# Windowed attention and a low-rank mixer in one kernel: the down-product in four partial sums, folded and copied to four row groups from batch 3 on

## The chip, the core and the metric

The kernel runs on one core of a Trainium2 chip. The metric is the device time of one execution in microseconds; several runs are given by their median. The profile is that of one execution, taken by the hardware profiler.

## What is computed

The reference, cut to what matters:

```python
# q, k, v: (8 batches, 8 heads, 576 positions, 64)
scores = 1 / sqrt(64) * q @ k.T          # kept where 0 <= row - column < 64
x = softmax(scores) @ v                  # per batch: 576 positions x 512 channels
# U: 576 x 32, V: 32 x 576, w_ch1: 512 x 2048, w_ch2: 2048 x 512
h = x.T @ U @ V                          # mixes positions, rank 32
u = x + h.T
out = u + relu(u @ w_ch1) @ w_ch2
```

The change is about `x.T @ U @ V`. The first product (the down-product) sums over all 576 positions and gives 32 x 512 numbers a batch; the second (the up-product) makes 576 x 512 numbers of them, which are added to x.

## The kernel before, in words

All matmul operands are bf16. The 8 x 576 = 4608 positions are cut in two ways. Attention and the mixing of positions go by batch (576 positions: four and a half tiles of 128). The two large matmuls go by chunk (512 positions: four tiles); there are nine chunks, `mlp(c)`. A batch therefore begins or ends in the middle of a tile: batch 3 covers tiles 13 (its second half) to 17, batch 4 tiles 18 to 22 (its first half), and so on.

The order of the work is written out by hand. Each engine has one queue, which it works off in the order in which the program emits instructions; SP's queue only issues DMAs, and POOL's mostly does. `mlp(c)` is a list of 32 slots of four 512-column matmuls: slots 0 to 15 are the first large product (`ch1`, tile `psA`, each followed by a relu on ACT or VectorE into `c1_i`), slots 16 to 31 the second (`ch2`, tile `psU`, four slots for each of the four tiles of the chunk). The last slot of a tile ends with an addition on VectorE (`osb`, L761) and the store of the result by SP (L774). The last loop of the program goes through the slots and emits after each what the table `PLACE` puts there for batch b = c + 1. So the work of batch 3 is spread over chunk 2, that of batch 4 over chunk 3, and so on to batch 7 in chunk 6; chunks 7 and 8 have no such work.

What the table places, with its slots for batches 3 to 7 before the change:

- `S`, `M`, `PV` (slots 0 to 8): scores, masks and the product with v; ends with the divisions on VectorE into `xs` (L487 to L510).
- `U` (slot 14), function `UM`, L531 and L539: the down-product. `ub` (128 positions x 32) is the stationary operand, so one matmul fills 32 of the array's columns, and the array takes four such matmuls beside each other (column groups g = 0 to 3, rows 32 g to 32 g + 31 of the result `pshh`). Tile t of the batch goes to the groups t % 2 and t % 2 + 2, both times over all 512 channels. The fifth, half-filled tile goes to all four groups, with 256 channels each. So rows 0 to 63 of `pshh` hold two partial sums which together are the result, and rows 64 to 127 hold the same again. ACT copies the whole to `hh` in bf16 (L546).
- `V` (slot 16), function `VM` by way of `mixed`, L619: the up-product. The stationary operand is `vrep`, which has V four times, once in each group of 32 rows. A matmul takes 64 rows of `hh` and of `vrep`, and so adds the two partial sums while it multiplies. Two matmuls lie beside each other (rows 0 to 63 and 64 to 127) with two results. There are three pairs: `(4,)` (256 columns each), `(0, 1)` and `(2, 3)` (512 columns each). Six additions on VectorE (L634) then put x plus the result into the tiles `un`.
- `UT` (slots 17, 17, 18, 18, 19): the transposed copies of `un` into `uTc`, the input of `ch1`. For batches 3 to 7 these are DMA transposes on SP's queue (L649). The first `ch1` of a chunk needs all four of its tiles: chunk 3 needs the first three of batch 3, chunk 4 the first two of batch 4, chunk 5 the first two of batch 5, chunks 6 and 7 one of batches 6 and 7.

Also on SP's queue: the DMA transposes of keys and queries for a later batch (`TX`, L304, slots 20 to 24 by `CROSS_N`, slots 24 to 28 in chunk 2). POOL issues the loads of keys, queries and values (L128, L137) for later batches. Within a slot the slot's own work comes first, then `S`, `M`, `PV`, then `TX`, then `U`, `V`, `UT`. PSUM: `pshh` and the pairs of V take from `ps_big` (two tiles of two banks); `psA`, `psU` and one tile of V take turns in three single banks.

Of the kernel before, what the change touches and what calls it, by code (L numbers as in the profile page):

```python
# [9 lines left out]
ALU = mybir.AluOpType  # L10

BF16 = mybir.dt.bfloat16
FP32 = mybir.dt.float32
# [3 lines left out]
def kernel(  # L17
# [11 lines left out]
    nc = tc.nc  # L29
    B, H, S, D = q.shape  # L30
    DM = H * D
    R = moe_U.shape[1]
    F = moe_w_ch1.shape[1]
    P = nc.NUM_PARTITIONS
# [7 lines left out]
    NGR = 2  # L42
    NXB = 2
    NXT = 3
    GP = S // GR
    NFULL = S // P
    CH = 512
# [15 lines left out]
    wk_pool = ctx.enter_context(tc.tile_pool(name="wk", bufs=2))  # L63
# [42 lines left out]
    def staged(b):  # L106
        if b >= NGR:
            return kn[b % 2], qn[b % 2]
        return tuple(
            r[0:GP, :].rearrange("p (h c d) -> p h c d", h=H, c=GR) for r in (kr[b % 2], qr[b % 2])  # L110
        )
# [38 lines left out]
    def shift_low(b, copy, t):  # L150
# [9 lines left out]
        out=ident[:],  # L160
        in_=ident[:],
# [10 lines left out]
    for n, base, step, mult in ((0, 0, 1, -1), (1, -1, -1, 1), (1, W, 1, -1)):  # L172
        nc.gpsimd.affine_select(
            out=maskA[:, 0, n, :],
            in_=maskA[:, 0, n, :],
# [17 lines left out]
    for i in range(2):  # L193
        nc.vector.memset(kn[i][GP:P, NFULL, :, :], 0.0)
        nc.vector.memset(qn[i][GP:P, NFULL, :, :], 0.0)


    nc.sync.dma_start(
        out=uf[0][:, 0:NFULL, :], in_=moe_U[0 : NFULL * P, :].rearrange("(c p) r -> p c r", p=P)
# [48 lines left out]
    def uT_of(c):  # L248
        if c not in uT_tiles:
            uT_tiles[c] = uT_pool.tile([P, TPC, NDC, P], BF16, name="uTc")  # L250
        return uT_tiles[c]


    def attention(b, spare=False):
# [9 lines left out]
        kx, qx = (f.rearrange("p (t j w) -> p t j w", t=NT, j=HP) for f in (kf, qf))  # L264

        grouped = b < NGR
        turn = [0]

        def tr(src, j, wide=False):
# [6 lines left out]
            else:  # L276
                tp = ps_tp.tile([P, GR, GP], BF16, name="tpg", tag="tp")
            turn[0] += 1
            for c in range(GR):
                for g in range(2):  # L280
                    nc.tensor.transpose(  # L281
                        tp[g * D : (g + 1) * D, c, :], src[:, 2 * j + g, c, :], ident[0:GP, 0:GP]
                    )
# [233 lines left out]
        hh = {}  # L517
        xc = lambda src, t, dc: src[:, t, :, :].rearrange("p h d -> p (h d)")[:, dc * P : (dc + 1) * P]

        def UM(ts):  # L520
            def f():
                if ts[0] == 0:
                    if spare:
                        hh["ps"] = psum["spare"].tile([P, CH], FP32, name="psh", tag="spare")
                    else:
                        hh["ps"] = ps_big.tile([P, 2, CH], FP32, name="pshh", tag="big")[:, 0, :]
                for t in ts:
                    xt = x[:, t, :, :].rearrange("p h d -> p (h d)")
                    if t < 4:
                        for g in (t % 2, t % 2 + 2):  # L530
                            nc.tensor.matmul(  # L531
                                hh["ps"][g * R : (g + 1) * R, :], ub[odd][:, t, :], xt,
                                start=(t < 2), stop=False,
                            )
                        continue

                    for g in range(4):
                        cols = slice((g % 2) * CH // 2, (g % 2 + 1) * CH // 2)
                        nc.tensor.matmul(  # L539
                            hh["ps"][g * R : (g + 1) * R, cols], ub[odd][:, t, :], xt[:, cols],  # L540
                            start=False, stop=True,
                        )
                if ts[-1] == NT - 1:
                    hh["sb"] = wk_pool.tile([P, CH], BF16, name="hh", tag="hh")
                    for cs in (slice(0, CH // 2), slice(CH // 2, CH)) if spare else (slice(0, CH),):
                        nc.scalar.copy(out=hh["sb"][:, cs], in_=hh["ps"][:, cs])  # L546
            return f
# [57 lines left out]
        def VM(ts, banks=None):  # L605
            ps = {}
            cols = CH if len(ts) == 2 else CH // 2

            def up():
                if banks is None:  # L610
                    pair = ps_big.tile([P, 2, CH], FP32, name="psv", tag="big")
                    ps[0] = [pair[:, n, 0:cols] for n in range(2)]
                else:
                    ps[0] = [one[:, 0:cols] for one in banks()]
                for n in range(2):
                    half = slice(n * 2 * R, (n + 1) * 2 * R)
                    off = ts[n % len(ts)] * P + (0 if odd else W)
                    lo = 0 if len(ts) == 2 else n * cols
                    nc.tensor.matmul(  # L619
                        ps[0][n], vrep[half, off : off + P], hh["sb"][half, lo : lo + cols],  # L620
                        start=True, stop=True,
                    )

            def add(n):
                def f():
                    t = ts[n % len(ts)]
                    g = g0 + t
                    rs = slice(
                        W if (odd and t == 0) else 0, W if (not odd and t == NT - 1) else P
                    )  # L630
                    cs = slice(0, CH) if len(ts) == 2 else slice(n * cols, (n + 1) * cols)
                    if g not in u_tiles:
                        u_tiles[g] = u_pool.tile([P, DM], BF16, name="un")
                    nc.vector.tensor_tensor(  # L634
                        out=u_tiles[g][rs, cs],
                        in0=ps[0][n][rs],
                        in1=x[rs, t, :, :].rearrange("p h d -> p (h d)")[:, cs],
                        op=ALU.add,
                    )
                return f  # L640

            return [up, add(0), add(1)]

        def UT(t):
            def f():
                g = g0 + t
                dst = uT_of(g // TPC)[:, g % TPC, :, :]
                if b >= NXT:
                    nc.sync.dma_start_transpose(out=dst, in_=u_tiles[g][:])  # L649
# [59 lines left out]
    def mlp(c):  # L709
# [80 lines left out]
        "M": [0, 1, 2, 4, 5],  # L790
        "PV": [8],
        "U": [14],
        "V": [16],
        "UT": [17, 17, 18, 18, 19],
    }
    PLACE_0 = {"V": [0, 0, 1, 2, 2, 3, 4, 4, 4]}
    PLACE_1 = {
# [29 lines left out]
    def turn_over(n, cols, rows=P):  # L827
# [5 lines left out]

    turn_over(62, 96)
    att = {0: attention(0, spare=True)}
    a = att[0]
    nc.vector.tensor_scalar(
        out=maskA[:, 0, 2, :],
        in0=maskA[:, 0, 1, :],
# [6 lines left out]
        out=maskB[:, 0:3, :],  # L846
        in0=maskA[:, 0, 0:3, :],
# [56 lines left out]
    for c in range(NCH):  # L904
        slots = all_slots[c]

        def place(b, parts, where):
            if b not in att:
                att[b] = attention(b)
            for part in parts:  # L910
                for f, s in zip(att[b][part], where[part]):
                    all_slots[c + s // 100][s % 100].append(f)

        b = c + 1
# [85 lines left out]
```

The softmax here doesn't subtract the row's maximum and nothing guards it: scores larger than these inputs give would overflow.

## Time and profile before

| what | value |
|---|---|
| median of 9 runs | 313.05 us (312.71 to 315.79) |
| the profiled execution's own time | 313.05 us |
| its span, first to last instruction | 311.3 us |
| granted TensorE clock, mean | 1.000 |
| `psA` L724, TensorE | 131.2 us busy, 580 matmuls |
| `psU` L748, TensorE | 129.1 us busy, 592 matmuls |
| `pshh` L531 and L539, TensorE, 7 batches | 4.3 us (56 of 512 columns) and 2.0 us (28 of 256) |
| `psv` L619, TensorE | 5.0 us (32 of 512 columns) and 2.3 us (16 of 256) |
| `hh` L546, ACT | 587 ns each, 7 times |
| `un` L634, VectorE | 26.1 us, 48 times |
| DMA transposes `uTc` from `un`, SP's queue | 23, median 6.7 us from issue to landing |

How to read it: a busy time is the union of the instructions of one kind, so matmuls that lie beside each other count once; the end of a matmul is modelled, so a matmul of 512 columns is shown as 378 ns although the next can start after 216. In the timeline a line is a run of instructions of one kind, with start and duration in us; in brackets stand the engine's idle time before it and what ended it. "SPq" is the time that the SP queue takes to issue a DMA; when it lands is told apart.

### The profile page before, as it was taken

The page shows a single profiled execution, that of the slowest core. Times are in us where ns is not written, and L with a number is a line of the kernel's source. Part 1 is how long each engine was busy: PE and PEld are TensorE (multiplying, and loading weights), DVE is VectorE, ACT ScalarE, POOL GpSimd, SP SyncE. Part 2 cuts the span into 40 slices and gives each one's busy share as a digit, 9 for nine tenths or more (in the row PEclk, how much of TensorE's full clock was granted, in tenths as well). Part 3 has the DMA queues.
Part 4 walks back from the last instruction along what each step waited for, and adds up shares of the span by engine and source line. Part 5 has one row for each costly group of instructions (what it writes and reads, how often), then busy time and mean ns, then how long its engine had stood idle before and what let it go on. Part 6 is the DMA issues. An engine that isn't in the chain of part 4 may idle for free.

```text
span 311.3 us, 6992 instructions
## 1 busy us (share of the span) xinstructions
PE 304.5 (98%) x2919; PEld 147.3 (47%) x2919; DVE 162.6 (52%) x308; ACT 108.9 (35%) x173; POOL 101.7 (33%) x133
## 2 busy tenths in 40 slices
PE   7899999999999999999999999999999999999996
PEld 6543554544455544454445344534454444444443
DVE  4575467437758754774368435844574343016011
ACT  3655670467038510642063304340345003201500
POOL 8693263294399097029307900000000000000000
PEclk9999999999999999999999999999999999999999
DMA  7999999999999999999999997505100545010012
GB/s 102 164 208 208 207 168 151 147 140 147 129 150 154 132 145 162 181 159 154 159 163 188 170 133 169 128 32 133 69 2 0 120 180 193 27 76 34 0 64 73
DMA packets 156496, 39.88 MB, mean 128 GB/s; under 512 B 145040, under 2 KB 151440, under 8 KB 156464
## 3 DMA queue, kind: packets, MB, share of 16 engines
q0 software_dynamic: 104720, 18.88, 83.3%
q1 hardware_dynamic: 51744, 20.55, 36.0%
q8 instruction: 23, 0.38, 0.5%
q14 instruction: 9, 0.07, 0.1%
HBM read 37.97 MB, written 9.44 MB: 152 GB/s over the span
## 4 chain that ended last, share of the span: by engine, by line
PE 93%; DMA 3%; POOL 2%; issue 0%; ACT 0%; DVE 0%; POOLq 0%
PE psA L724 41%; PE psU L748 40%; DMA vA<-in_v_dram 3%; PE sc L345 3%; PE xw L407 2%; PE psv L619 2%; PE pshh L531 1%; PE tpu L653 1%; PE tpg L281 0%; POOL qr L119 0%; PE low L345 0%; PE psh L531 0%; POOL vB L151 0%; PE xr L407 0%; POOL kr L119 0%
## 5 line engine op out<-in xcount | busy, mean ns | idle before, releaser
L724 PE MATMUL psA<-uTc,w1b 128*128 128x512 bf16 (+1 forms) x580 | 131.2, 378 | 0.4 <-ACT uTc L599 0.4
L748 PE MATMUL psU<-w2b,c 128*128 128x512 bf16 (+2 forms) x592 | 129.1, 373 | 0.0
L748 PEld LDWEIGHTS <-c 128*128 128x128 bf16 x592 | 56.0, 98 | 66.4 <-issue 3.6
L724 PEld LDWEIGHTS <-w1b 128*128 128x128 bf16 x580 | 54.1, 98 | 64.4 <-issue 2.9
L736 ACT ACTIVATE c<-psA 128x512 bf16<-128x512 f32 x84 | 50.1, 597 | 88.3 <-PE psA L724 88.0
L761 DVE TENSOR_TENSOR osb<-psU,un 128x512 f32<-128x512 f32 (+2 forms) x29 | 19.5, 673 | 68.9 <-PE psU L748 68.9
L734 DVE TENSOR_SCALAR c<-psA 128x512 bf16<-128x512 f32 x60 | 41.4, 689 | 25.6 <-PE psA L724 25.6
L634 DVE TENSOR_TENSOR un<-psv,xs 128x512 bf16<-128x512 f32 (+3 forms) x48 | 26.1, 593 | 23.2 <-PE psv L619 22.9
L365 ACT ACTIVATE pts<-sc 128x1024 bf16<-128x1024 f32 x32 | 31.4, 1029 | 2.4 <-PE sc L345 2.3
L137 POOL DMA_DIRECT2D vA<-in_v_dram x32 | 28.4, 912 | 7.7 <-DMA kr<-in_k_dram 3.0
L128 POOL DMA_DIRECT2D qr<-in_q_dram x30 | 26.6, 887 | 3.8 <-PE sc L345 1.8
L128 POOL DMA_DIRECT2D kr<-in_k_dram x30 | 26.5, 883 | 3.5 <-PE tpg L281 2.0
L398 ACT ACTIVATE ptl<-low 128x256 bf16<-128x256 f32 x6 | 2.3, 384 | 62.0 <-PE high L345 62.0
L371 DVE TENSOR_TENSOR pts<-pts,maskA 128x1024 bf16<-128x1024 bf16 x28 | 19.1, 683 | 1.7 <-ACT pts L365 1.7
L922 POOL COPY held<-qf 1x1 bf16<-1x1 bf16 x5 | 0.9, 179 | 53.1 <-DMA qf<-qr 43.5
L498 DVE TENSOR_TENSOR xs<-xw,rcw 128x896 bf16<-128x896 f32 x14 | 15.3, 1092 | 0.5
L345 PEld LDWEIGHTS <-kf 64*64 64x64 bf16 x704 | 9.8, 107 | 7.6 <-issue 7.0
L345 PE MATMUL sc<-qf,kf 64*64 64x128 bf16 (+1 forms) x608 | 11.5, 212 | 0.5 <-DVE qf L298 0.3
L407 PEld LDWEIGHTS <-pts 128*64 128x64 bf16 x512 | 9.9, 110 | 3.6 <-issue 3.0
L546 ACT CAST hh<-pshh 128x512 bf16<-128x512 f32 x7 | 4.1, 587 | 13.6 <-PE pshh L539 13.5
L656 ACT COPY uTc<-tpu 128x512 bf16<-128x512 bf16 x9 | 5.3, 586 | 10.2 <-PE tpu L653 10.2
L137 POOL DMA_DIRECT2D vB<-in_v_dram x8 | 7.4, 922 | 3.4 <-DMA qr<-in_q_dram 2.4
(115 smaller groups left out, 175.8 us busy)
## 6 DMA issues: line engine op xcount, KB each, us to landing
out_dram<-osb SPq DMA_DIRECT2D x27, 256.0 KB, 2.3
vA<-in_v_dram POOLq DMA_DIRECT2D x32, 128.0 KB, 8.5
kr<-in_k_dram POOLq DMA_DIRECT2D x24, 128.0 KB, 6.1
qr<-in_q_dram POOLq DMA_DIRECT2D x24, 128.0 KB, 6.3
w2b<-in_moe_w_ch_dram POOLq DMA_DIRECT2D x4, 512.0 KB, 15.7
out_dram<-late SPq DMA_DIRECT2D x8, 256.0 KB, 3.0
vB<-in_v_dram POOLq DMA_DIRECT2D x8, 128.0 KB, 10.5
w1b<-in_moe_w_ch_dram POOLq DMA_DIRECT2D x2, 512.0 KB, 10.9
```

Source lines behind the costliest of these rows:

```text
L128: nc.gpsimd.dma_start(out=dst[0:rows, t, :, :], in_=src[b, :, t * P : t * P + rows, :].rearrange("h p d -> p h d"),)
L137: nc.gpsimd.dma_start(out=dst[:, :, 0:D], in_=v[b, :, lo : lo + P, :].rearrange("h p d -> p h d"))
L345: nc.tensor.matmul(sc[g][r0 : r0 + W, col * W : (col + n) * W], keys_of(j, u, rs), queries_of(j, blk, n, rs), start=not spare, stop=last o ...
L365: nc.scalar.activation(out=dst, in_=sc[:], func=ACT.Exp, scale=scale)
L371: nc.vector.tensor_tensor(out=dst, in0=dst, in1=maskA.rearrange("p g n w -> p g (n w)"), op=ALU.mult)
L407: nc.tensor.matmul(dst, pts[:, h // 2, h % 2, blk, :] if blk < NB - 1 else ptl[:, h // 2, h % 2, :], rhs, start=True, stop=True,)
L634: nc.vector.tensor_tensor(out=u_tiles[g][rs, cs], in0=ps[0][n][rs], in1=x[rs, t, :, :].rearrange("p h d -> p (h d)")[:, cs], op=ALU.add,)
L724: nc.tensor.matmul(ps[i][:, ts.start * P : ts.stop * P], w1b[:, dc, i * P : (i + 1) * P], uTc[:, ts, dc, :], start=(dc == 0), stop=(dc == ...
L734: nc.vector.tensor_relu(out=c1[i][:], in_=ps[i][:])
L736: nc.scalar.activation(out=c1[i][:], in_=ps[i][:], func=ACT.Relu)
L748: nc.tensor.matmul(acc[t][:, lo:hi], c1[i][:, t * P : (t + 1) * P], w2b[:, i, lo:hi], start=(i == 0), stop=(i == NFC - 1),)
L761: nc.vector.tensor_tensor(out=osb[:, lo:hi], in0=acc[t][:, lo:hi], in1=u_tiles[g][:, lo:hi], op=ALU.add,)
```

## The change

From batch 3 on (`folded`, with `NFOLD = 3`):

- Down-product: tile t goes to column group t alone, so one wave of four matmuls replaces two; the fifth tile goes to all four groups with 128 channels each. `pshh` then holds four partial sums.
- Instead of one copy by ACT: ACT copies rows 64 to 127 to `part` in fp32; VectorE adds rows 0 to 63 to it, copies rows 32 to 63 of that to `other`, adds both into rows 0 to 31 of `hh` in bf16, and copies these to rows 32 to 63 and then rows 0 to 63 to rows 64 to 127.
- Up-product: a matmul takes 32 rows. The pair `(4,)` uses row groups 0 and 1, the pair `(0, 1)` groups 0 and 1, the pair `(2, 3)` groups 2 and 3.
- The table: V from slot 16 to 18, UT from 17, 17, 18, 18, 19 to 19, 19, 20, 20, 21.

```diff
+    NFOLD = 3
...
+        folded = b >= NFOLD
...
                     if t < 4:
-                        for g in (t % 2, t % 2 + 2):
+                        for g in (t,) if folded else (t % 2, t % 2 + 2):
                             nc.tensor.matmul(
                                 hh["ps"][g * R : (g + 1) * R, :], ub[odd][:, t, :], xt,
-                                start=(t < 2), stop=False,
+                                start=(folded or t < 2), stop=False,
                             )
                         continue
 
                     for g in range(4):
-                        cols = slice((g % 2) * CH // 2, (g % 2 + 1) * CH // 2)
+                        n = 4 if folded else 2
+                        cols = slice((g % n) * CH // n, (g % n + 1) * CH // n)
...
                     hh["sb"] = wk_pool.tile([P, CH], BF16, name="hh", tag="hh")
+                    if folded:
+                        one, two = slice(R, 2 * R), slice(0, 2 * R)
+                        part = wk_pool.tile([2 * R, CH], FP32, name="part", tag="part")
+                        other = wk_pool.tile([R, CH], FP32, name="other", tag="other")
+                        nc.scalar.copy(out=part[:], in_=hh["ps"][2 * R : P])
+                        nc.vector.tensor_tensor(
+                            out=part[:], in0=hh["ps"][two], in1=part[:], op=ALU.add
+                        )
+                        nc.vector.tensor_copy(out=other[:], in_=part[one])
+                        nc.vector.tensor_tensor(
+                            out=hh["sb"][0:R], in0=part[0:R], in1=other[:], op=ALU.add
+                        )
+                        nc.vector.tensor_copy(out=hh["sb"][one], in_=hh["sb"][0:R])
+                        nc.vector.tensor_copy(out=hh["sb"][2 * R : P], in_=hh["sb"][two])
+                        return
...
                     half = slice(n * 2 * R, (n + 1) * 2 * R)
+                    if folded:
+                        q = ts[n] if len(ts) == 2 else n
+                        half = slice(q * R, (q + 1) * R)
...
-        "V": [16],
-        "UT": [17, 17, 18, 18, 19],
+        "V": [18],
+        "UT": [19, 19, 20, 20, 21],
```

## The prediction, made before the changed kernel ran

> **What bounds the kernel now.** I read the page first: engine shares and the chain that ended last.
> ```profile
> PE 304.5 (98%) x2919; PEld 147.3 (47%) x2919; DVE 162.6 (52%) x308; ACT 108.9 (35%) x173; POOL 101.7 (33%) x133
> ...
> PE 93%; DMA 3%; POOL 2%; issue 0%; ACT 0%; DVE 0%; POOLq 0%
> ```
> TensorE bounds it; its DMA and POOL shares of the chain lie in the first 20 us. Every microsecond taken off TensorE is a gain, unless a wait takes its place. So I next read batch 3 (the first changed one, in chunk 2) in order of time. TensorE and ACT:
> ```profile
> 108.57 0.62 PE L531 MATMUL pshh<-xs,ub 128*32 128x512 bf16 x8
> 109.02 0.28 PE L539 MATMUL pshh<-xs,ub 128*32 128x256 bf16 x4
> 109.23 1.04 PE L724 MATMUL psA<-uTc,w1b 128*128 128x512 bf16 x4
> 110.10 1.03 PE L748 MATMUL psU<-w2b,c 128*128 128x512 bf16 x4
> 111.06 0.71 PE L619 MATMUL psv<-hh,vrep 64*128 64x256 bf16 x6
> 111.71 0.60 PE L748 MATMUL psU<-w2b,c 128*128 128x512 bf16 x2
> ```
> ```profile
> 108.68 0.60 ACT L736 ACTIVATE c<-psA 128x512 bf16<-128x512 f32 x1 [0.27 <-PE psA L724]
> 109.35 0.59 ACT L546 CAST hh<-pshh 128x512 bf16<-128x512 f32 x1
> ```
> Columns: start, duration, engine and line. The down-product (U) holds TensorE from 108.57 to 109.23, the up-product (V) from 111.06 to 111.71. Then VectorE and the SP queue, on which the transposes `uTc<-un` of the next chunk stand:
> ```profile
> 111.38 3.40 DVE L634 TENSOR_TENSOR un<-psv,xs 128x256 bf16<-128x256 f32 x6 [3.93 <-PE psv L619]
> 114.70 0.68 DVE L761 TENSOR_TENSOR osb<-psU,un 128x512 f32<-128x512 f32 x1
> ```
> ```profile
> 112.89 6.00 SPq L649 DMA_TRANSPOSE uTc<-un  x4
> 118.99 0.53 SPq L774 DMA_DIRECT2D out_dram<-osb  x1
> 119.58 1.33 SPq L649 DMA_TRANSPOSE uTc<-un  x1
> 121.00 0.54 SPq L774 DMA_DIRECT2D out_dram<-osb  x1
> 121.64 1.27 SPq L304 DMA_TRANSPOSE kf<-kr  x1
> ```
> The first three of these transposes by the view of the tile uTc, and the start of chunk 3 on TensorE:
> ```profile
> L649 SPq DMA_TRANSPOSE uTc<-un x3: 1207/1245/1471, 112.9 to 115.6; - x3
> ...
> DMA to landing us min/median/max: 6.2/7.2/7.9
> ```
> ```profile
> 124.67 1.03 PE L724 MATMUL psA<-uTc,w1b 128*128 128x512 bf16 x4
> ```
> Chunk 3 multiplies tiles 12 to 15, and batch 3's first three transposes make 13, 14 and 15. The third lands at 115.6 + 7.9 = 123.5, only 1.2 us before TensorE wants it. This margin is hidden from the list of waits, and it decides the case.
>
> **What the change takes off TensorE.** I count from U's start (108.57 = 0). U is two waves of four 512-column matmuls, 0.22 apart, then a wave of 256 columns (0.11) and 0.10 until the next matmul in another array shape: 0.66. After: one wave of four (0.22), one of 128 columns (0.05), 0.10: 0.39. That is -0.27. V is 0.12 + 0.22 + 0.22 + 0.10 = 0.65. After, the pairs of `(0,1)` and `(2,3)` lie on different row groups and run together, while the pair of `(4,)` shares groups 0 and 1 with `(0,1)`: 0.12 + 0.22 + 0.01 + 0.10 = 0.45, -0.20. Five batches: 5 x 0.47 = -2.4 us.
> The trace has four column tiles at once (the four starts of a wave lie within 0.01 us), but of row tiles only two. The Trainium skill speaks against the full gain: "TensorE: Matmul & The Clock Gate", Measured speedup vs the span model, gives four row tiles of 512 columns 3.07 times. With 0.38 for one matmul that is 4 x 0.38 / 3.07 = 0.49 in place of 0.39, so V saves 0.10, and the sum is -1.9 us. I take the row: pairs start within 0.01 us and the next pair 0.22 later. If nothing more than now runs together, U keeps only its smaller last wave: -0.05 a batch, -0.3 in all. A loss has no cause there: there are fewer matmuls and as many changes of shape.
>
> **The fold, and when V can start.** TensorE reaches V at 0.39 (U) + 0.87 (c_15) + 12 x 0.216 (slots 16 to 18 of psU) + 0.10 = 3.95. The fold: ACT's copy keeps its place and length (a 64-row copy of 512 fp32; the row above, 0.59) and ends at 109.94, 1.37. The handover ACT to VectorE is 0.03 (ptl in this trace), between dependent VectorE operations 0.03 (rce to xs), back to TensorE 0.05. Add of PSUM and SBUF: 0.69 (`osb` rows). Copy of 512 fp32 in SBUF: no such row; between a 520-element bf16 copy (0.28) and an fp32 one out of PSUM (0.69). "VectorE: DVE Perf Modes", The perf-mode tier table, has fp32 copies at 2x, 1227 ns for 2048, from which I estimate 0.43, and take it. Second add: 0.69 (same form; the page has fp32 adds at 1x too). Two bf16 copies: 0.28 each. Sum 1.37 + 0.03 + 0.69 + 0.43 + 0.69 + 0.56 + 4 x 0.03 + 0.05 = 3.94. So without disturbance V waits for nothing, and the cover is gone to the last 0.01 us: whatever is longer is on the path. VectorE itself is idle there (3.93 us idle before un).
> The disturbance is in the trace. The SBUF copies of VectorE are longer while POOL issues DMAs:
> ```profile
> L144 DVE COPY vB<-vA x1: 830/830/830, 118.7 to 118.7; 64x1560 bf16<-64x1560 bf16 x1
> ```
> ```profile
> L144 DVE COPY vB<-vA x1: 565/565/565, 182.8 to 182.8; 64x1560 bf16<-64x1560 bf16 x1
> ```
> Over eleven such copies the excess goes from 0 to 0.38, mean 0.13. POOL issues during the fold of batches 3, 4 and 5, not of 6 and 7: three copies, +0.39 (bounds 0 and 1.1). There V starts at 4.34. Alone, the change would then give 3 x (0.39 - 0.47) + 2 x (-0.47) = -1.2.
> The PSUM pair of pshh is held until the first add (2.1) instead of 1.37; V asks for it after 3.9, so nothing waits. The bank of psU t=2 is free when the first `osb` add is done (8.66 below), and slot 24 wants it at 4.34 + 0.45 + 0.87 + 4 x 0.864 = 9.1: covered by 0.4.
>
> **What is late next: the transposes.** V moves from slot 16 to 18 and UT from 17..19 to 19..21. Slot 19's own work ends with the first `osb` add of the chunk and its store, which are emitted ahead of the slot's extras. In the built order of the SP queue the store therefore stands now ahead of all five transposes, and it waits for VectorE, which does six `un` adds first. Batch 3: V 4.34, first add 0.32 later (111.06 to 111.38), adds and osb 4.00 (111.38 to 115.38): 8.66. Handover 0.1, store's issue 0.59: first transpose at 9.35, where it was at 4.32. From first issue to third landing the trace has 112.9 to 123.5, 10.6: lands at 19.95. TensorE wanted it at 124.67 - 108.57 = 16.1. Chunk 3 begins **3.9 us later** than before (gain and fold included).
> Can it land sooner? Unloaded, in chunk 5, four transposes land 2.4 us after their issue, so three would take 2 x 1.3 + 2.4 = 5.0, and nothing would stall:
> ```profile
> L649 SPq DMA_TRANSPOSE uTc<-un x4: 1191/1212/1218, 208.9 to 212.8; - x4
> ...
> DMA to landing us min/median/max: 2.4/2.4/2.4
> ```
> But POOL issues key, query and value loads until 124.2 and the page's DMA row stays at 9 till 187 us. The loads outstanding at 118 are not fewer than at 113. Nearest row: 10.6; bounds 5.0 and 12.
> Batch 4 needs two (tiles 18 and 19). V 4.34 + 0.32 + 3.83 (143.42 to 147.25) + 0.1 + 0.65 = 9.24; first issue to second landing 144.8 to 153.3, 8.5: 17.7 against 16.1, +1.6. The loads for batch 6 follow the SP queue, which lags by 3.5 where TensorE lags by 3.9, so they are 0.4 ahead: I take **+1.4** (0 to 2). Batch 5 needs two, but its loads are all issued by 178.9, 6.2 after U's start, and gone when the transposes come at 9.2: no stall, -0.1. Batches 6 and 7 need one, unloaded: -0.47 each. On SP the key and query transposes of the batch after next are now woven in behind the second one; these are wanted a chunk later and have over 10 us to spare.
> Sum: 3.9 + 1.4 - 0.1 - 0.9 = **+4.3**. The profiled execution has a span of 311.3 and a time of 313.05, which is also the median of the runs. So a span of 315.6 and a time near 317.3; I say 317.2.
>
> **Rivals.** (1) *Transposes in time* (0.12). One mechanism: with SP silent from 113 to 118 the loads run ahead alone and the late transposes meet a free DMA. It decides where first issue to third landing is under 16.0 - 9.35 = 6.7. For it: 5.0 unloaded; against it: from 101 to 180 us every transpose took 5.5 us or more but for three issued between 162 and 166. Then the sum is -1.2: 311.9. With some of the delay: 312.5 to 315.5 (0.13, of it 0.05 under 314.0). (2) *Likeliest* (0.63): 315.5 to 318.7. (3) *The clock too* (0.07). TensorE would idle 4.0 us ahead of chunk 3. After the start its longest idle stretch in this trace is under 1 us, with PEclk at 9. "TensorE: Matmul & The Clock Gate", What's actually happening, lets an idle window of about 3.4 us halve the clock until a busy one has passed. By the row nothing happens; by the rule, as the windows run free, (4.0 - 3.4) / 3.4 = 0.18 of cases lose about half of 3.4 us, 1.7: 318.9. (4) *It does not pack* (0.05). U is 0.61 and V 0.65. Chunks 3 and 4 begin as above, since the transposes set them and V still waits for the fold; batch 5 gives 4.34 - 4.17 - 0.05 = +0.1, 6 and 7 -0.05 each: +5.3, 318.3.
>
> **Range.** 313.4 to 319.0: leaves out rival 1, a little of what lies between, and half of 3: 0.18. A measurement of this kernel tells 0.3% (0.9 us) from no change: faster 0.12, same 0.05, slower 0.83.
>
> **What would show it.** U's block 0.39 and V's 0.45 on TensorE; five VectorE operations between U and V, 2.6 to 3.1 us from end to end of the fold; the first `uTc<-un` 9 us after U, behind the store of osb; TensorE idle of some 4 us at the start of chunk 3 and 1.5 at chunk 4, released by DMA uTc, none at chunk 5 and later. Wrong if those transposes land within 6.7 us, or if the fold takes much over 3.1 us: then V itself is the wait, five times.

## The result, and the profile after

The changed kernel takes 318.39 us (median of 10 runs, 316.42 to 319.36), the kernel before 313.15 us in the same sessions (31 runs). The ratio is 1.0152, with a 95% interval of 1.0134 to 1.017: slower, by 4.8 us by the ratio and 5.2 by the medians. The profiled execution took 317.36 us, its span is 315.7.

The page of the changed kernel, its engine shares, slices, chain of waits and costliest group. Line numbers are some 21 higher than before (`psA` is L745, `psU` L769, `psv` L640, `un` L655, `uTc` L670):

```profile
PE 306.0 (97%) x2899; PEld 148.6 (47%) x2899; DVE 174.3 (55%) x333; ACT 108.7 (34%) x173; POOL 102.1 (32%) x133
...
PEclk9999999999999999599999999999999999999999
DMA  7999999999999999999957998651500166020012
...
PE 89%; DMA 5%; POOL 2%; DVE 1%; SPq 1%; issue 1%; ACT 0%; POOLq 0%
...
L745 PE MATMUL psA<-uTc,w1b 128*128 128x512 bf16 (+1 forms) x580 | 133.1, 382 | 4.1 <-DMA uTc<-un 3.7
```

TensorE is busy for longer (306.0, before 304.5) although it has 20 matmuls fewer, and 3.7 us of idle time ahead of `psA` are new, released by a transpose. The 5 in the row PEclk, slice 17 of 40 counted from 1, is the reason for the longer busy time: the granted clock was halved there. In the DMA row, slices 21 and 22 (158 to 174 us) are at 5 and 7, where they were at 9.

Batch 3 in order of time, first TensorE, then VectorE, then the SP queue, then the start of chunk 3:

```profile
108.46 0.40 PE L533 MATMUL pshh<-xs,ub 128*32 128x512 bf16 x4
108.69 0.23 PE L542 MATMUL pshh<-xs,ub 128*32 128x128 bf16 x4
108.85 1.04 PE L745 MATMUL psA<-uTc,w1b 128*128 128x512 bf16 x4
109.72 2.75 PE L769 MATMUL psU<-w2b,c 128*128 128x512 bf16 x12
112.41 0.62 PE L640 MATMUL psv<-hh,vrep 32*128 32x256 bf16 x6
```

```profile
111.72 0.28 DVE L560 COPY hh<-hh 32x512 bf16<-32x512 bf16 x1
112.03 0.55 DVE L561 COPY hh<-hh 64x512 bf16<-64x512 bf16 x1
```

```profile
116.72 0.37 SPq L795 DMA_DIRECT2D out_dram<-osb  x1
117.15 7.18 SPq L670 DMA_TRANSPOSE uTc<-un  x5
```

```profile
128.08 1.87 PE L745 MATMUL psA<-uTc,w1b 128*128 128x512 bf16 x4 [3.72 <-DMA uTc<-un]
```

U takes 0.39 from its start to the next matmul (0.66 before). V starts 3.95 after U without a wait on TensorE. The store of the first `osb` stands ahead of the transposes, as foreseen; the first transpose goes at 117.15, 8.69 after U (4.32 before). The third lands at 119.82 + 8.12 = 127.94, and 0.14 later chunk 3 begins, 19.62 after U where it was 16.10. Its first four matmuls take 1.87 us in place of 1.03: they run at half clock. TensorE in stretches of 3.41 us (start and end, length, then busy time and count of TensorE, weight loads, VectorE, ACT and POOL, the granted clock, and two columns that are not used here):

```profile
123.06:126.47 3.41, 1.30 (x7) 0.39 (x4) 0.69 (x1) 0.00 (x0) 0.00 (x0) 1.00 2.12 148
126.47:129.88 3.41, 1.80 (x5) 0.44 (x5) 0.00 (x0) 0.00 (x0) 0.00 (x0) 0.50 1.82 134
129.88:133.29 3.41, 3.41 (x59) 1.91 (x59) 1.39 (x3) 2.49 (x4) 0.00 (x0) 0.50 1.22 256
```

The wait begins at 128.08 - 3.72 = 124.36. The clock falls 2.1 us later and stays at a half for 6.83 us; from 128.08 to 133.29 TensorE works at half speed. What that costs can be read between the start of chunk 3 (128.08, before 124.67) and U of batch 4, a stretch in which nothing was changed:

```profile
140.62 0.61 PE L531 MATMUL pshh<-xs,ub 128*32 128x512 bf16 x8
```

```profile
146.44 0.40 PE L533 MATMUL pshh<-xs,ub 128*32 128x512 bf16 x4
```

It is 15.95 us before and 18.36 after: the half clock costs 2.4 us. Laid side by side, the stretches of the two kernels give this account (start of U in batch 3 to chunk 3, then chunk to chunk, in us):

| stretch | before | after | difference | predicted |
|---|---|---|---|---|
| U of batch 3 to chunk 3 | 16.10 | 19.62 | +3.52 | +3.9 |
| chunk 3 to 4 (batch 4) | 32.04 | 34.26 | +2.22 | +1.4 |
| chunk 4 to 5 (batch 5) | 32.05 | 31.71 | -0.34 | -0.1 |
| chunk 5 to 6 (batch 6) | 32.04 | 31.56 | -0.48 | -0.47 |
| chunk 6 to 7 (batch 7) | 32.04 | 31.55 | -0.49 | -0.47 |

The sum is +4.43; U of batch 3 itself comes 0.11 sooner, so +4.3, and the spans differ by 315.7 - 311.3 = 4.4. The +2.22 of batch 4 is +2.41 for the clock, ahead of its U, and -0.19 behind it.

### The profile page after: what moved, and what is told of

Its sections match the earlier page's. It is cut to its first block, busy times and chain, and to the rows that moved or that the text cites. A ratio compares the mean times of both kernels' runs of the same rounds, so it can differ in the third digit from the quotient of the medians.

```text
span 315.7 us, 6956 instructions
## 1 busy us (share of the span) xinstructions
PE 306.0 (97%) x2899; PEld 148.6 (47%) x2899; DVE 174.3 (55%) x333; ACT 108.7 (34%) x173; POOL 102.1 (32%) x133
## 4 chain that ended last, share of the span: by engine, by line
PE 89%; DMA 5%; POOL 2%; DVE 1%; SPq 1%; issue 1%; ACT 0%; POOLq 0%
PE psA L745 41%; PE psU L769 36%; DMA vA<-in_v_dram 3%; PE sc L347 3%; DMA uTc<-un 3%; PE xw L409 2%; PE psv L640 1%; DVE un L655 1%; PE pshh L533 1%; SPq L670 1%; PE tpu L674 1%; PE tpg L283 0%; PE low L347 0%; POOL qr L120 0%; POOL vB L152 0%
## 5 line engine op out<-in xcount | busy, mean ns | idle before, releaser
L745 PE MATMUL psA<-uTc,w1b 128*128 128x512 bf16 (+1 forms) x580 | 133.1, 382 | 4.1 <-DMA uTc<-un 3.7
L769 PE MATMUL psU<-w2b,c 128*128 128x512 bf16 (+2 forms) x592 | 129.1, 373 | 0.0
L745 PEld LDWEIGHTS <-w1b 128*128 128x128 bf16 x580 | 54.5, 99 | 69.2 <-issue 8.7
L769 PEld LDWEIGHTS <-c 128*128 128x128 bf16 x592 | 55.9, 98 | 65.7 <-issue 2.8
L655 DVE TENSOR_TENSOR un<-psv,xs 128x512 bf16<-128x512 f32 (+3 forms) x48 | 26.1, 593 | 4.6 <-PE psv L640 4.2
L553 DVE TENSOR_TENSOR part<-pshh,part 64x512 f32<-64x512 f32 x5 | 3.4, 683 | 12.6 <-ACT part L552 12.6
L782 DVE TENSOR_TENSOR late<-psU,un 128x512 f32<-128x512 f32 x8 | 5.3, 688 | 5.8 <-PE psU L769 5.7
```

Source lines behind the costliest of these rows:

```text
L655: nc.vector.tensor_tensor(out=u_tiles[g][rs, cs], in0=ps[0][n][rs], in1=x[rs, t, :, :].rearrange("p h d -> p (h d)")[:, cs], op=ALU.add,)
L745: nc.tensor.matmul(ps[i][:, ts.start * P : ts.stop * P], w1b[:, dc, i * P : (i + 1) * P], uTc[:, ts, dc, :], start=(dc == 0), stop=(dc == ...
L769: nc.tensor.matmul(acc[t][:, lo:hi], c1[i][:, t * P : (t + 1) * P], w2b[:, i, lo:hi], start=(i == 0), stop=(i == NFC - 1),)
L782: nc.vector.tensor_tensor(out=osb[:, lo:hi], in0=acc[t][:, lo:hi], in1=u_tiles[g][:, lo:hi], op=ALU.add,)
```

## The experiments

The theory: the move of V and UT makes the transposes late (chunk 3 waits), the wait makes the clock fall, and packing and fold gain a little in each batch. The rival: the fold itself, its VectorE work or the contention that it meets, costs the time.

**The move alone.** The kernel before, with only the table changed:

```diff
-        "V": [16],
-        "UT": [17, 17, 18, 18, 19],
+        "V": [18],
+        "UT": [19, 19, 20, 20, 21],
```

> The kernel before with V in slot 18 and UT in 19 to 21, without the fold and the four partial sums. Theory (late transposes): the first transpose goes 9 to 9.6 us after U's start, chunk 3 begins 4 us late, the clock halves for one or two windows (1.6 to 2.2 us), and nothing is gained: 319 (318.3 to 320). Rival (the fold or its contention is the cost): 313 to 313.5, as before.

Measured: 318.81 us, ratio 1.0193 (1.0173 to 1.0212). Without any fold, the start of chunk 3 looks as after:

```profile
127.72 1.86 PE L724 MATMUL psA<-uTc,w1b 128*128 128x512 bf16 x4 [3.10 <-DMA uTc<-un]
```

Chunk 3 begins 19.36 after U, +3.26; chunk 3 to 4 lasts 34.72, +2.68; the later chunks last 32.04 as before. The clock falls here too (0.50, the third column from the right):

```profile
126.64:133.47 6.83, 5.75 (x63) 2.57 (x64) 1.94 (x4) 2.49 (x4) 0.00 (x0) 0.50 1.29 194
```

Nothing but the clock is left to explain the 2.68, since nothing is packed here and no wait stands in that stretch. So the move alone costs 317.1 - 311.3 = 5.8 us of span, more than the whole change, and the rival falls.

**The transposes ahead of the store.** The changed kernel, with the first store of chunks 2 to 6 held back until the slot of the last UT is through:

```diff
-                    nc.sync.dma_start(out=outf[g * P : (g + 1) * P, lo:hi], in_=osb[:, lo:hi])
+                    store = lambda: nc.sync.dma_start(
+                        out=outf[g * P : (g + 1) * P, lo:hi], in_=osb[:, lo:hi]
+                    )
+                    if t == 0 and HOLD <= c + 1 < B:
+                        behind.append(store)
+                        continue
+                    store()
...
             for f in extra:
                 f()
+            if behind and fill is ups_21:
+                behind.pop(0)()
```

> Theory (late transposes): the loss is the transposes of un standing behind the first osb store on the SP queue. With that store behind them, the first one goes at about 6.3 us after U's start (third un add done) in place of 8.7, the third lands some 10.8 later at 17.1, and TensorE wants it at 15.5: 1.6 us of idle ahead of chunk 3, too short for half a clock, so a time of 312.7 (311.2 if the transposes also land sooner, 314 if they land later). Clock 1.0. Rival (the fold, its VectorE work or the place of V is the cost): no change, 317 to 318.5.

Measured: 312.4 us, ratio 0.9975 (0.9958 to 0.9992), 6 us under the changed kernel. The first transpose goes 6.04 after U, and what is left of the wait is small:

```profile
114.76 7.60 SPq L672 DMA_TRANSPOSE uTc<-un  x5
```

```profile
125.46 1.02 PE L747 MATMUL psA<-uTc,w1b 128*128 128x512 bf16 x4 [0.46 <-DMA uTc<-un]
```

The order on the SP queue, with what follows from it, is thus by far the most of the loss. The runs go from 310.98 to 316.01, where those of the kernel before in the same sessions go from 312.67 to 315.31. The margin is near zero, and how fast the transposes land differs between executions: in the six traces in which batch 3 is as before, the third takes 6.6 to 8.1 us. That this makes the spread is likely, but the other runs have no trace.

**The clock.** The changed kernel, with matmuls on a zero tile in the wait of chunk 3, into the bank which the first real matmul then overwrites (17 of them, in the next kernel 8):

```diff
+                if (c, ids) == (3, (0,)):
+                    for _ in range(17):
+                        nc.tensor.matmul(
+                            ps[0], idle[:, 0:P], idle[:, 0:CH], start=True, stop=True
+                        )
```

> The changed kernel with 17 matmuls on the zero tile ahead of chunk 3's first matmul, in the same bank, which the first real matmul overwrites; they fill some 3.7 us in which TensorE waits for the transposes. Theory (idleness halves the clock): chunk 3 begins as late as after (within 0.3), the granted clock is 1.0, and the time is 316.4 (316.0 to 316.9), 1.6 to 2.2 less than after. Rival (the half clock follows from something else in that stretch): clock 0.99 as before, 318.4 or a little more.

Measured: 315.86 us, ratio 1.0092 (1.0071 to 1.0112), less than after, while TensorE does 3.7 us of extra work. In its profiled execution chunk 3 begins 19.54 after U, as late as after, and the clock is full ahead of it and behind it. (The 17 matmuls end last here. The third transpose had landed two microseconds earlier, so that without them only some 1.7 us would have been idle: this trace alone proves little.)

```profile
123.00:130.50 7.50, 7.50 (x36) 3.43 (x35) 1.38 (x2) 0.00 (x0) 0.00 (x0) 1.00 1.66 185
130.50:137.00 6.50, 6.50 (x113) 3.25 (x111) 4.02 (x7) 4.40 (x7) 0.00 (x0) 1.00 0.56 105
```

The five other runs have a mean clock of 0.999 or 1.000; the 0.993 of the profiled one comes mostly from a half-clock stretch from 14.6 to 18.0, in the start of the program. So all eleven executions of the changed kernel lose clock, and with the wait filled none of six does there. The idle wait is what halves the clock, and that was worth some 2 us here (2.5 by the medians, 0.006 of 313 = 1.9 by the ratios).

> As busy_wait with 8 matmuls on the zero tile in place of 17: 1.7 us of the wait are filled, some 2.1 stay idle. After, the half clock began 2.3 us into an idle of 3.9. If a window has to be idle for most of 3.4 us, clock 1.0 and 316 as with 17. If 2 us of idle are enough, clock 0.995 and 317.5 (2.6 to 3.4 us at half clock, less what is already idle).

With 8: 316.33 us, ratio 1.0091 (1.0062 to 1.0121), neither of the two answers. Three of six runs have a clock of 0.995 and take 316.9 to 317.4, three have 0.999 or 1.000 and take 314.6 to 315.7. In the profiled one the transposes landed late, 2.85 us stayed idle, and the clock fell for 3.41 us. The two expectations had not allowed for both outcomes in one kernel; whether the length of the wait or its place decides between them, these runs do not show.

**The fold from batch 4 on.** Batch 3 keeps the old products and the old slots:

```diff
-    NFOLD = 3
+    NFOLD = 4
...
-    PLACE_3 = {**PLACE, "SV": [5, 5, 6, 6]}
+    PLACE_3 = {**PLACE, "SV": [5, 5, 6, 6], "V": [16], "UT": [17, 17, 18, 18, 19]}
```

> The change from batch 4 on; batch 3 as in the kernel before, with its old slots. Chunk 3 then begins as before, clock 1.0. If chunk 4's transposes stall as predicted for batch 4 (+1.4), the time is 313.1 + 1.4 - 0.1 - 0.9 = 313.5. If they do not, as in the changed kernel, four batches give 0.45 each: 311.3. Rival (the fold itself costs time): over 313.5.

Measured: 312.37 us, ratio 0.9984 (0.997 to 0.9999), between the two, with runs from 310.77 to 315.19. The two transposes that chunk 4 needs, and its start, in the profiled execution (312.06 us):

```profile
L670 SPq DMA_TRANSPOSE uTc<-un x2: 1283/1540/1797, 149.5 to 150.8; - x2
...
DMA to landing us min/median/max: 5.7/6.2/6.8
```

```profile
156.93 1.03 PE L745 MATMUL psA<-uTc,w1b 128*128 128x512 bf16 x4
```

They land at 156.3 and 156.5, 0.4 us ahead of TensorE: just in time here, and so probably late in the longer runs (one of them has a clock of 0.994), which have no trace. With the store also held back (both edits, from batch 4 on), that chance should go:

> The change from batch 4 on, and in its chunks the first osb store behind the transposes of un on the SP queue. With the fold from batch 4 on alone the two transposes of batch 4 landed 0.4 us before chunk 4 in the profiled run, and the runs spread from 310.8 to 315.2. Theory (these transposes are late by chance in some runs): they go 1.8 us sooner, no chunk waits, four batches give 0.45 each: 311.3, spread under 1.5 us. Rival (the spread comes from the fold): 312.4 as without it.

Measured: 311.73 us, ratio 0.9952 (0.994 to 0.9964), runs from 311.59 to 312.08. The five runs lie within 0.5 us. That fits late transposes as the source of the spread, and not the fold, but five runs are few: `fold_4_act_copy` below, in which the store is held back too, goes from 311.91 to 314.52 in 22. This version beats both kernels, by 1.6 us the one before.

**The fold from batch 5 on**, with `NFOLD = 5` and the old slots for batches 3 and 4:

> The change from batch 5 on only; batches 3 and 4 as in the kernel before with their old slots. No transposes of these batches fall into the loads' time. If packing and fold are worth what the periods of chunks 5 and 6 show after (0.48 each), three batches give 1.4: 311.7, with little spread and clock 1.0. Rival (part of what a batch gained after came from the loads having run ahead in the stall): 312.5 to 313.

Measured: 312.02 us, ratio 0.9961 (0.9948 to 0.9974), 1.3 under the 313.33 of the kernel before beside it; 1.4 was expected. Chunks 5 and 6 last 31.56 each, as in the changed kernel, so the gain of a quiet batch doesn't hang on the stall of chunk 3. Chunk 4 to 5 lasts 31.88: batch 5 gives only 0.17.

**Two row groups or four.** The same with all pairs of V on row groups 0 and 1, and without the last copy of `hh`:

```diff
-                        q = ts[n] if len(ts) == 2 else n
+                        q = n
...
-                        nc.vector.tensor_copy(out=hh["sb"][2 * R : P], in_=hh["sb"][two])
```

> The fold from batch 5 on, with all pairs of V on the first two row groups, and so without the last copy of hh. It measures what the four row groups give V. By the row of before (pairs on the same groups 0.22 apart) V is 0.65 again, and chunks 6 and 7 last 31.77 us where four groups give 31.56 and the kernel before 32.04: 0.21 between two and four groups, 312.5 in all. By the rule of 3.07 times the difference is 0.10, chunks 6 and 7 at 31.66. If the row groups give nothing, 31.56. Batch 5, whose third pair waited for the last copy, is then no slower than with four groups.

Measured: 312.21 us, ratio 0.9988 (0.9968 to 1.0007); by the time alone this is unclear, by the trace it isn't. Chunks 5 and 6 last 31.78 and 31.77, 0.21 more than with four groups. V of batch 6 on TensorE, first with two groups, then with four (`fold_from_5`):

```profile
208.37 0.71 PE L639 MATMUL psv<-hh,vrep 32*128 32x256 bf16 x6
209.01 0.82 PE L768 MATMUL psU<-w2b,c 128*128 128x512 bf16 x3
```

```profile
208.74 0.50 PE L640 MATMUL psv<-hh,vrep 32*128 32x256 bf16 x6
209.17 0.60 PE L769 MATMUL psU<-w2b,c 128*128 128x512 bf16 x2
```

Start to start 0.64 and 0.43: the four row groups give what the row of before said (0.65 and 0.45), not half of it. Batch 5 lasts 31.88, the same as with four groups: V's block is 0.76 in both, since in both the first copy of `hh` took 0.72 there (0.28 in batches 6 and 7) and V waited for it and, with four groups, for the copy behind it.

**V in its old slot.** The changed kernel with V in slot 16 and UT in 17 to 19:

> The changed kernel with V in slot 16 and UT in 17 to 19, as before. TensorE reaches V at 0.39 + 0.87 + 4 x 0.216 + 0.1 = 2.2 us after U, the fold is ready at 3.95: a wait of 1.75 in each of five batches, 8.7 us. The transposes then go ahead of the osb store and land near 17 us after U, where TensorE wants them at 15.7 + 1.75: no stall, clock 1.0. 313.1 - 2.4 + 8.7 = 319.4. Rival (the fold's wait is short or is taken back before the next chunk): under 315.

Measured: 320.7 us, ratio 1.0223 (1.0203 to 1.0243). The tile `psv` shows the wait:

```profile
  DVE hh L557: 5.3, 5
```

Five waits of 1.06 on average, released by the second add (L557) and not by the copies behind it: V's first matmul reads rows 0 to 31 of `hh` only, and starts 3.3 to 3.5 after U. The second, which elsewhere starts at the same moment, follows 0.3 to 0.4 later, after the copy to rows 32 to 63. Each wait is thus shorter than the 1.75 expected. Without a fall of the clock a batch lasts 33.2, 1.1 longer than before; but four of the five runs also lost clock, which had not been expected. So the later slot is needed for the fold, and leaving V where it was costs more than the move.

**The last copy on ACT**, in the best version (`fold_4_ut_first`):

```diff
-                        nc.vector.tensor_copy(out=hh["sb"][2 * R : P], in_=hh["sb"][two])
+                        nc.scalar.copy(out=hh["sb"][2 * R : P], in_=hh["sb"][two])
```

> The fold from batch 4 on with the store behind the transposes, and the last copy of hh (64 rows) on ACT in place of VectorE. Theory (POOL's DMA issues lengthen the SBUF copies of VectorE alone): the copy takes the same in batches 4 and 5 as in 6 and 7, some 0.5 us, and the excess of 0.26 is seen no more in this copy; since an undisturbed copy of VectorE takes 0.28, the time stays at 311.7 to 312.2. Rival (any SBUF copy beside POOL's issues is longer): ACT's copy is longer in batch 4 or 5 than in 6 and 7 by 0.2 or more.

Measured: 312.76 us, ratio 0.9992 (0.9978 to 1.0006). The tile `hh`, ACT's copy and VectorE's before it (ns, shortest, median, longest):

```profile
L563 ACT COPY hh<-hh x4: 616/616/617, 144.6 to 240.5; 64x512 bf16<-64x512 bf16 x4
```

```profile
L562 DVE COPY hh<-hh x4: 283/416/734, 143.8 to 240.2; 32x512 bf16<-32x512 bf16 x4
```

ACT's copy takes the same in all four batches, while VectorE's copy ahead of it takes 734 and 550 in batches 4 and 5, in which POOL issues DMAs, and 283 in 6 and 7. As far as two copies can show it, the excess belongs to VectorE's copies within SBUF. The time was mis-expected: the third pair waits for ACT in all four batches. V's block is 0.64 in batches 6 and 7 in place of 0.43, and 1.09 and 1.31 in 4 and 5, where VectorE's longer copies come on top. (Of the 2.9 us by which the span of this execution exceeds that of `fold_4_ut_first`, half lies behind the issue of the last store, where nothing was changed.)

## Why the prediction was right, and where its sum was not

**Direction, place and size held.** The predicted 317.2 is close to the profiled 317.36, and the range holds the median of 318.39. What bounds the kernel, the order on the SP queue and the stall of chunk 3 were read off the trace of before. But two terms of the sum, batch 4 and the clock, were wrong by about 2 us each and cancelled. That the total is so close is luck; the stall of chunk 3 is not.

**TensorE's gain** was right: U 0.39; V 0.43 in batches 6 and 7, which gave 0.48 and 0.49 for a predicted 0.47. For packing by row groups the trace's row held. The smaller gain was an estimate from the 3.07 times that the Trainium skill gives for four row tiles ("TensorE: Matmul & The Clock Gate", Measured speedup vs the span model); it would have made V 0.55.

**The fold** has the foreseen parts: 0.58 (ACT), 0.68, 0.42 (estimated at 0.43), 0.68, 0.28, 0.28 undisturbed. Wrong was "There V starts at 4.34": it starts at 3.95 in every batch. The prediction took `hh` for one thing that is ready or not; a matmul waits only for the rows it reads, and only the pair on the third and fourth row groups needs the last copy. The excess was real (the last copy took 554, 689 and 555 ns in batches 3, 4 and 5, and 287 and 289 in 6 and 7), but cost TensorE only the wait of the third pair: V's block is 0.55, 0.72 and 0.58 in batches 3, 4 and 5 against 0.43 in the quiet ones.

**The transposes of batch 3** were right: first one at 8.69 for 9.35 (the 0.39 of V is most of it), 10.8 to the third landing for 10.6, chunk 3 later by 3.5 for 3.9. `place_only` and `ut_first` show the cause from both sides.

**Batch 4, "+1.4", failed.** There was no stall: from U of batch 4 to chunk 4 it takes 15.90, 0.19 less than before. The step that failed is "The loads for batch 6 follow the SP queue, which lags by 3.5". The queue did lag by 3.5: the key and query transpose on whose landing POOL waits was issued at 129.23 before and at 132.77 now. But it landed 8.1 us behind its issue before, and 4.0 in the changed kernel, so POOL's wait ended earlier and the loads did not lag. Before, then after:

```profile
129.23 1.28 SPq L304 DMA_TRANSPOSE qf<-qr  x1
```

```profile
137.47 0.18 POOL L922 COPY held<-qf 1x1 bf16<-1x1 bf16 x1 [13.28 <-DMA qf<-qr]
137.98 0.88 POOL L128 DMA_DIRECT2D kr<-in_k_dram  x1 [0.33 <-issue]
```

```profile
132.77 2.06 SPq L306 DMA_TRANSPOSE qf<-qr  x1
```

```profile
136.85 0.18 POOL L943 COPY held<-qf 1x1 bf16<-1x1 bf16 x1 [14.96 <-DMA qf<-qr]
137.36 0.88 POOL L129 DMA_DIRECT2D kr<-in_k_dram  x1 [0.34 <-issue]
```

The prediction moved the issue and kept the landing time. Why this transpose landed sooner no run isolates. TensorE had meanwhile fallen 5.8 us behind (U of batch 4 at 146.44, before at 140.62), so the loads were nearly through when the transposes went, at 154.9 and 156.2:

```profile
L670 SPq DMA_TRANSPOSE uTc<-un x2: 1213/1235/1257, 154.9 to 156.2; - x2
...
DMA to landing us min/median/max: 2.5/2.7/2.9
```

That is close to the 2.4 us of an idle DMA. The first stall paid for the second, and not by the clock alone: in `busy_wait`, where chunk 3 is as late but the clock stays full, the two land at 159.3 and 159.8, and chunk 4 begins 31.56 after chunk 3. `fold_from_4` takes the first stall away, and there the same transposes take 5.7 to 6.8 and chunk 4 has 0.4 us left: even so the +1.6 first worked out for this batch (from 8.5 to the second landing, where 7.0 was measured) was too much for that execution.

**The clock** was the other wrong term. The main case put it at nothing; the rival gave it 0.18 of the cases, by asking for a window of 3.4 us that is wholly idle. It happened in every one of the eleven recorded executions (mean clock 0.989 or 0.995), and cost 2.4 in the profiled one. "By the row nothing happens" had no support, since the trace of before has no such stretch. The rule of the Trainium skill ("TensorE: Matmul & The Clock Gate", What's actually happening) was the better guide: half-clock stretches of 3.41 us (`busy_half`) and 6.83 us fit one and two of its windows of about 3.4 us. Only "idle" was read too strictly: the window ahead of the fall, if it ends where the fall begins, still had 1.30 us of work in 3.41.

In all, against the sum: chunk 3 -0.4, batch 4 -1.6, batch 5 -0.2, clock +2.4, together +0.2. The profiled execution is one of the shorter ones; the median lies 1 us above it.

## What to carry to other kernels

When a step is moved, write out the queue on which its DMAs stand: a store that waits for an addition, put ahead of the transposes, cost here 3.5 us at a margin of 1.2. A margin that no list of waits shows, third landing against first use, is the number to look for; it decides how far something may be moved. An idle stretch of TensorE of 3 to 4 us cost more than itself here: behind waits of 3.1 and 3.7 us the half clock took another 2.4 to 2.7.

## What had not been expected of the hardware

- A stretch need not be empty for the clock to fall. In `fold_old_slots` one in which TensorE was busy for 2.08 of 3.41 us was followed by half clock; part of that work was V's matmuls of 32 rows. If the trace is laid out in stretches of 3.41 us through that fall, the four like it in the other batches hold 2.27 to 2.36 us of work, and no fall follows. That is no clean threshold: in `fold_4_act_copy`, in stretches laid through its fall at the end, one with 1.95 us (306.25 to 309.66) has none behind it. What the measure of activity is, these runs do not settle.

```profile
176.81:180.22 3.41, 2.08 (x12) 0.61 (x11) 3.21 (x8) 0.14 (x1) 2.25 (x3) 1.00 2.44 154
180.22:183.64 3.42, 3.42 (x10) 1.18 (x9) 2.35 (x4) 0.00 (x0) 0.00 (x0) 0.50 2.39 115
```

- A DMA transpose of this size lands in 2.4 to 2.9 us on a DMA that is idle or nearly so, and the five of batch 3 in the changed kernel took 6.7 to 8.7 us beside the loads. A kernel whose margin is near zero varied by 5 us from run to run (`ut_first`, 22 runs, two of which lost clock, 0.993).
- VectorE's copies within SBUF took up to 3 times as long while POOL issued DMAs (848 ns for 283 in `busy_wait`); VectorE's additions (0.68) and ACT's copy (616 ns) did not change. Over the ten traces with a fold, all 29 of its copies that are lengthened by more than 20 ns overlap such an issue, and the 59 copies that overlap none keep their length; but 34 overlap one and keep it too. That the issues are the cause is inferred from this; no run moved them.
- TensorE did not start the three pairs of V in the order in which they are emitted. Where nothing is late (batches 6 and 7) pairs start at 0, 0.01 and 0.12 us. The one at 0.01 must be the third: the second has the row groups of the first, and pairs on the same groups start 0.12 apart. Where the last copy is late (batch 3 of the changed kernel) the starts are 0, 0.12 and 0.23, with the third last. So the queue of TensorE is not worked off quite in the order of emission.
